# A half-sample Fourier basis with folded mirror tiles, and mask tables built two slots earlier, in a fused attention and long-convolution kernel

## The chip, the cores and the metric

The kernel runs on one core of one Trainium2 chip. The metric is the device time of one execution in microseconds (us). The granted clock is the share of PE's full clock that the profile shows as allowed. Engines are PE (TensorE), PEld (its weight loads), DVE (VectorE), ACT (ScalarE), POOL (GpSimd) and SP (SyncE).

A ratio below is the mean time of one kernel's fast runs over that of the other kernel's fast runs of the same rounds, so it is not quite the ratio of the medians quoted beside it. Brackets hold its 95% interval. An execution counts as slow when it is over 1.5% above the fastest of the same kernel.

## The reference

```python
# q, k, v: (4, 8, 768, 64); heads are "retrieval" (causal) or "stream" (4 sinks + window of 64)
scores = np.where(mask, scale * q @ k.T, -1e9);  a = softmax(scores)
x = (a @ v).transpose(0, 2, 1, 3).reshape(4, 768, 512)
proj = x @ w_proj;  x1, x2, x3 = split(proj, 3)              # 512 columns each
X2 = rfft(x2, axis=1);  H = rfft(filter_fft, axis=0)         # length 768
y = x1 * irfft(X2 * H) * x3
out = y @ w_out
```

## The kernel before

Sixteen pairs of heads (four batches of four) go through slots `n` = 0 to 15. In each slot the attention of one pair runs beside steps of the convolution of the batch before. Up to `n == 4` the engines' queues keep the order of the code. From slot 5 on a scheduler places what is emitted for PE, DVE and ACT, and it may put an instruction ahead of older ones when its operands allow. GpSimd and SyncE keep the order of the code throughout.

The Fourier transform is a matrix product. Tokens t and t+384 are added and subtracted, which leaves 3 tiles of 128 rows for each spectrum tile. So there are 6 output tiles x 3 matmuls = 18 forward matmuls a batch. The filter's spectrum tables HA and HB come from the same transform, straight from PSUM with a scale.

```python
psum = ctx.enter_context(tc.tile_pool(name="psum", bufs=4, space=bass.MemoryType.PSUM))   # 4 bank pairs
# ...
def emit_kinds():                        # which of three mask kinds, 128x3x256
    nc.vector.tensor_copy(out=kinds[:, 0:2], in_=code)
    nc.vector.tensor_copy(out=kinds[:, 2, 0:128], in_=code[:, 1, 0:128])
    nc.vector.memset(kinds[:, 2, 128:256], 2.0)
def emit_mask(h):                        # one table for each head
    nc.vector.tensor_scalar(out=mask[:, h], in0=kinds, scalar1=least[:, h:h + 1], scalar2=None, op0=ALU.is_ge)
# ...
def setup_steps():                       # filter tables, cut into steps by yield
    # fold = sum and difference of the filter's halves (DVE) ... yield
    ps = emit_forward(fold, ((0, 0), (1, 0)))
    for out_, in_, w in (...):           # four ACT copies with a scale: HA[:, 0], HB[:, 0]
        nc.scalar.activation(out=out_, in_=in_, func=AF.Copy, scale=scales[:, w:w + 1])
    put(nc.scalar, HA[0:1, 0, 1, :], ps[0:1, 1], 1.0)
    yield
    # tile 1: three DVE scales; yield; tile 2: one DVE and one ACT scale
# ...
for m in range(NM):                      # moe: x2 = projection, then sums and differences of the halves
    # 8 matmuls, x2s = ACT copy of the bank
    nc.vector.tensor_add(x2[:, 0, m, :], x2s[:, 0], x2s[:, 1])
    nc.vector.tensor_sub(x2[:, 1, m, :], x2s[:, 0], x2s[:, 1])
# ...
if n == BIASED:                          # BIASED = 4: the fifth pair's slot
    emit_turn(state[n - 2]); emit_values(last); emit_norm(last)
    emit_kinds(); emit_mask(0); emit_mask(1)
    next(setup); emit_turn(last); next(setup)
    emit_masking(st, 0); emit_chunks(st, 1); gates.append(moe(b - 1, last["xT"]))
    # ...
if n < 2 * BIASED:                       # slots 5 to 7
    emit_mask(2 * hp); emit_mask(2 * hp + 1)
```

The softmax here doesn't subtract the row's maximum and nothing guards it: scores larger than these inputs give would overflow.

Of the kernel before, what the change touches and what calls it, by code (L numbers as in the profile page):

```python
# [44 lines left out]
def kernel(  # L45
# [81 lines left out]
    def emit_prep(st):  # L127
        st["qkT"] = qkT = asb.tile([128, 2, S], BF16, name="qkT", bufs=3)
        if st["n"] < BY_PE:
            ps = bank_pair("qkT_ps", BF16)  # L130
            for a in range(2):
                for t in range(NT):
                    nc.tensor.transpose(ps[:, a, t * 128:(t + 1) * 128],
                                        st["bf"][:, a, t].rearrange("p hh d -> p (hh d)"), identity)
                if st["n"] == 0:
                    emit_blank(6 if a else 3)
            dst = qkT.rearrange("d a (p t) -> d a p t", t=NT)
            src = ps[:, :, 0:S].rearrange("d a (t p) -> d a p t", t=NT)
            if st["n"] == 0:
                for a in range(2):  # L140
                    nc.vector.tensor_copy(out=dst[:, a], in_=src[:, a])
            elif st["n"] <= BIASED:
                nc.vector.tensor_copy(out=dst, in_=src)
            else:
                nc.scalar.copy(out=dst, in_=src)
            return
        st["turn"] = nc.sync.dma_start_transpose(
            out=qkT.rearrange("p a (t s) -> p (a t) s", t=NT),
            in_=st["bf"].rearrange("p a t hh d -> p (a t hh d)"))
# [6 lines left out]
    def emit_blank(count):  # L156

        for i in range(count):
# [12 lines left out]
    tcol = const.tile([128, NM], FP32, name="tcol")  # L171
    nc.gpsimd.iota(tcol, pattern=[[128, NM]], base=0, channel_multiplier=1,
                   allow_small_or_imprecise_dtypes=True)
# [6 lines left out]
    nc.gpsimd.iota(par, pattern=[[0, 1]], base=0, channel_multiplier=1)  # L180
    nc.vector.tensor_scalar(out=par, in0=par, scalar1=1, scalar2=None, op0=ALU.bitwise_and)

    scales = const.tile([128, 4], FP32, name="scales")
    nc.gpsimd.memset(scales[:, 0:2], 2.0 / S)
    nc.gpsimd.memset(scales[:, 2:3], -2.0 / S)
    nc.gpsimd.memset(scales[0:1, :], 0.0)
    nc.gpsimd.memset(scales[0:1, 1:2], 1.0 / S)
    nc.gpsimd.memset(scales[0:64, 3:4], -2.0 / S)
    nc.gpsimd.memset(scales[64:128, 3:4], 2.0 / S)
    tfrac = const.tile([128, NM], FP32, name="tfrac")  # L190
    nc.vector.tensor_scalar(out=tfrac, in0=tcol, scalar1=1.0 / S, scalar2=None, op0=ALU.mult)
    quarter = const.tile([128, 1], FP32, name="quarter")
    nc.vector.memset(quarter, ETA * (S // 4))


# [14 lines left out]
    if n_sink:  # L210
# [3 lines left out]
        pattern=[[0, 2], [1, 128]], channel_multiplier=-1,  # L214
    )

    turns = msb.tile([128, NM, HS], I32, name="turns", tag="P")
# [8 lines left out]
    for m in range(NM):  # L226
        nc.vector.scalar_tensor_tensor(out=angle[:, m], in0=turns[:, m], scalar=-float(S),
                                       in1=angle[:, m], op0=ALU.mult, op1=ALU.add)
    nc.vector.tensor_scalar(out=size.bitcast(I32), in0=angle.bitcast(I32), scalar1=0x7fffffff,
                            scalar2=None, op0=ALU.bitwise_and)  # L230
    for out_, in_ in ((G[:, 1:4:2], angle[:, :, 0:256]), (G2[:, :, :, 64:128], angle[:, :, 256:384])):
        nc.scalar.activation(out=out_.rearrange("p r m f -> p m r f"), in_=in_.rearrange("p m (r f) -> p m r f", r=2), func=AF.Sin,
                             scale=-ETA)
    for out_, in_ in ((G[:, 0:4:2], size[:, :, 0:256]), (G2[:, :, :, 0:64], size[:, :, 256:384])):
        nc.scalar.activation(out=out_.rearrange("p r m f -> p m r f"), in_=in_.rearrange("p m (r f) -> p m r f", r=2), func=AF.Sin,
                             scale=-ETA, bias=quarter)
    emit_prep(state[0])
# [71 lines left out]
    def setup_steps():  # L309
        filt = state["filt"]  # L310
        fold = msb.tile([128, 2, NM, DM], BF16, name="fold", tag="y", bufs=2)
        nc.vector.tensor_add(fold[:, 0], filt[:, 0:NM, :], filt[:, NM:NT, :])
        nc.vector.tensor_sub(fold[:, 1], filt[:, 0:NM, :], filt[:, NM:NT, :])
        yield

        def put(engine, out, in_, w):
            if engine is nc.scalar:
                engine.activation(out=out, in_=in_, func=AF.Copy, scale=w / S)  # L318
            else:
                engine.tensor_scalar(out=out, in0=in_, scalar1=w / S, scalar2=None, op0=ALU.mult)  # L320


        ps = emit_forward(fold, ((0, 0), (1, 0)))
        for out_, in_, w in ((HA[:, 0, 0, :], ps[:, 0], 1), (HA[:, 0, 1, :], ps[:, 0], 0),
                             (HB[:, 0, 0, :], ps[:, 1], 2), (HB[:, 0, 1, :], ps[:, 1], 0)):
            nc.scalar.activation(out=out_, in_=in_, func=AF.Copy, scale=scales[:, w:w + 1])
        put(nc.scalar, HA[0:1, 0, 1, :], ps[0:1, 1], 1.0)
        yield
        ps = emit_forward(fold, ((2, 1), (3, 1)))
        put(nc.vector, HA[:, 1], ps[:, 0, None, :].to_broadcast([128, 2, DM]), 2.0)  # L330
        put(nc.vector, HB[:, 1, 0, :], ps[:, 1], -2.0)
        put(nc.vector, HB[:, 1, 1, :], ps[:, 1], 2.0)
        yield
        put(nc.vector, HA[:, 2], emit_forward(fold, ((4, 0), (5, 1))), 2.0)
        yield
        nc.scalar.activation(out=HB[:, 2], in_=emit_forward(fold, ((6, 0), (7, 1))), func=AF.Copy, scale=scales[:, 3:4])
        yield
# [71 lines left out]
    def emit_turn(st):  # L409
        if st["n"] < BY_PE or st["pair"][1] == HP - 1:  # L410
            ps = bank_pair("xt_ps", BF16)[:, 0, 0:S]
            for i in range(NT):
                nc.tensor.transpose(ps[:, i * 128:(i + 1) * 128],
                                    st["attn"][:, i].rearrange("p hh d -> p (hh d)"), identity)
            nc.vector.tensor_copy(out=st["xT"][:, st["pair"][1], :], in_=ps)  # L415
        else:
            nc.sync.dma_start_transpose(
                out=st["xT"][:, st["pair"][1], :].rearrange("p (t s) -> p t s", t=NT),
                in_=st["attn"].rearrange("p t hh d -> p (t hh d)"))


    def moe(b, xT):
        x2 = msb.tile([128, 2, NM, DM], BF16, name="x2")
        for m in range(NM):
            ps = bank_pair("x2_ps")
            for half in range(2):
                for cc in range(NC):
                    nc.tensor.matmul(ps[:, half, :], lhsT=xT[:, cc, half * HS + m * 128:half * HS + (m + 1) * 128],  # L428
                                     rhs=wproj[:, cc, DM:2 * DM],
                                     start=(cc == 0), stop=(cc == NC - 1))  # L430
            x2s = msb2.tile([128, 2, DM], BF16, name="x2s")
            nc.scalar.copy(out=x2s, in_=ps)  # L432
            nc.vector.tensor_add(x2[:, 0, m, :], x2s[:, 0], x2s[:, 1])
            nc.vector.tensor_sub(x2[:, 1, m, :], x2s[:, 0], x2s[:, 1])
            yield
        P = msb.tile([128, 3, 2, DM], BF16, name="P")
# [38 lines left out]
        def multiply(t, X):  # L475
            if t == 2:
                swapped = msb.tile([128, 2, DM], BF16, name="swapped")
                nc.sync.dma_start(out=swapped[0:64], in_=X[64:128])
# [10 lines left out]
        for t in range(3):  # L489
            X = msb2.tile([128, 2, DM], BF16, name="X", bufs=3)  # L490
            ps = emit_forward(x2, ((0, 0), (1, 1)), G2) if t == 2 else emit_forward(x2, ((2 * t, t), (2 * t + 1, t)))
            nc.scalar.copy(out=X, in_=ps)
# [113 lines left out]
    for n, (b, hp) in enumerate(pairs):  # L606
        if hp == 0:
            xT = msb.tile([128, NC, S], BF16, name="xT", bufs=2)
        st, last, nxt = state[n], state.get(n - 1), state.get(n + 1)
        st["xT"] = xT  # L610
        if n == MANUAL:
# [10 lines left out]
        if n < BIASED:  # L622
# [5 lines left out]
            else:  # L628
                setup = setup_steps()
                next(setup)  # L630
            emit_chunks(st, 1)
            if last:
# [6 lines left out]
            if n == 1:  # L639
                emit_doubles()  # L640
            continue
        if n == BIASED:
            emit_turn(state[n - 2])
            emit_values(last)
            emit_norm(last)
            emit_kinds()
            emit_mask(0)
            emit_mask(1)
            next(setup)
# [3 lines left out]
            emit_chunks(st, 1)  # L653
            gates.append(moe(b - 1, last["xT"]))
            gate_step()
# [27 lines left out]
        if hp == 0:  # L683
            gates.append(moe(b - 1, last["xT"]))
        if n != 2 * BIASED - 1:
# [14 lines left out]
    emit_turn(last)  # L700
    gates.append(moe(B - 1, xT))
    while gates:
# [38 lines left out]
```

## Time and profile before

| | before |
|---|---|
| median, range (the three runs before the prediction) | 214.45 us, 212.71 to 214.8 |
| profiled run | span 210.5 us, clock 0.992 of full speed |
| busy PE / DVE / ACT / POOL | 192.6 / 158.6 / 147.7 / 71.1 us |
| first x2 projection / first x1 projection on PE | 40.03 / 50.41 us |

In the lines of single instructions the columns are start, us, engine, line, operation, output and inputs, shapes, count, and in brackets the idle time before and what ended it.

### The profile page before, as it was taken

How to read it: one execution, taken by the hardware profiler on the slowest of the kernel's cores; microseconds unless marked ns; L12 is line 12 of the kernel's file. 1: busy time of each engine (PE TensorE's matmuls, PEld its weight loads, DVE VectorE, ACT ScalarE, POOL GpSimd, SP SyncE). 2: the span in 40 equal slices, each digit the busy share in tenths (PEclk: the TensorE clock that was granted, in tenths of full speed). 3: DMA queues.
4: the chain of work that ended last, by engine and by line, in shares of the span. 5: the costliest groups of instructions: out<-in, count | busy, mean ns of one | idle time of the engine just before them, and what ended most of it. 6: DMA issues, size and time to landing. Idle time of an engine off the chain costs nothing.

```text
span 210.5 us, 4337 instructions
## 1 busy us (share of the span) xinstructions
PE 192.6 (91%) x1763; PEld 106.2 (50%) x1763; DVE 158.6 (75%) x254; ACT 147.7 (70%) x183; POOL 71.1 (34%) x110
## 2 busy tenths in 40 slices
PE   7889998898969989999979999999899999999991
PEld 2346766444536546454536455545464654555540
DVE  6647877996899598996997777868975854686370
ACT  7798886896783777598857888789668246634621
POOL 6689365902482077255261520830000000000000
PEclk9999999999978999999999999999999999999999
DMA  5999998998999999997979799961403330022426
GB/s 154 251 311 234 292 271 202 184 199 158 216 196 180 222 206 180 229 241 133 219 137 205 162 213 242 246 114 23 90 0 111 118 112 0 3 50 91 186 73 250
DMA packets 89940, 35.29 MB, mean 168 GB/s; under 512 B 80320, under 2 KB 86464, under 8 KB 89920
## 3 DMA queue, kind: packets, MB, share of 16 engines
q1 hardware_dynamic: 87024, 32.13, 70.8%
q0 software_dynamic: 2896, 2.88, 8.6%
q8 instruction: 14, 0.23, 0.5%
q14 instruction: 6, 0.05, 0.1%
HBM read 24.65 MB, written 6.29 MB: 147 GB/s over the span
## 4 chain that ended last, share of the span: by engine, by line
PE 53%; DVE 24%; DMA 7%; ACT 6%; SPq 3%; POOL 3%; issue 2%; ACTq 0%; DVEq 0%; POOLq 0%
PE x_ps L444 17%; PE out_ps L533 9%; PE x_ps L428 8%; DMA qk_f<-in_k_dram 7%; PE c_ps L460 6%; PE att L395 5%; PE sc L362 4%; PE X_ps L301 3%; DVE pT L384 3%; DVE P L483 3%; SPq L95 3%; DVE attn L406 3%; ACT pT L377 3%; DVE mask L272 2%; DVE m L484 2%
## 5 line engine op out<-in xcount | busy, mean ns | idle before, releaser
L377 ACT ACTIVATE pT<-sc 128x1024 bf16<-128x1024 f32 x96 | 82.8, 922 | 16.3 <-PE sc L362 12.9
L444 PE MATMUL x_ps<-xT,wproj 128*128 128x384 bf16 x256 | 47.2, 334 | 3.6 <-DVE y L498 2.1
L115 POOL CAST qk_bf<-qk_f 128x768 bf16<-128x768 f32 x31 | 28.9, 939 | 63.1 <-DMA qk_f<-in_q_dram 55.8
L384 DVE TENSOR_TENSOR pT<-pT,mask 128x1024 bf16<-128x1024 bf16 x36 | 28.7, 797 | 12.0 <-ACT pT L377 12.0
L444 PEld LDWEIGHTS <-wproj 128*128 128x128 bf16 x256 | 24.8, 100 | 23.4 <-issue 7.7
L362 PE MATMUL sc<-qkT 64*128 64x512 bf16 (+3 forms) x256 | 28.0, 307 | 5.4 <-DVE xT L415 2.3
L395 PEld LDWEIGHTS <-pT 128*128 128x128 bf16 x672 | 23.1, 97 | 2.5 <-DVE pT L384 0.3
L395 PE MATMUL att<-v_aug,pT 128*128 128x65 bf16 x352 | 23.7, 193 | 0.0
L428 PE MATMUL x_ps<-wproj,xT 128*128 128x512 bf16 x96 | 22.1, 379 | 0.4 <-ACT HAB L318 0.2
L533 PE MATMUL out_ps<-wout,y 128*128 128x512 bf16 x92 | 21.8, 379 | 0.3 <-ACT pT L377 0.2
L452 ACT CAST x1s<-x_ps 128x768 bf16<-128x768 f32 x16 | 12.8, 801 | 11.7 <-PE x_ps L444 10.4
L395 PE MATMUL att<-v_far,pT 128*128 128x65 bf16 x320 | 20.7, 193 | 0.0
L362 PEld LDWEIGHTS <-qkT 64*128 64x128 bf16 x256 | 9.7, 94 | 19.5 <-issue 13.9
L347 POOL TENSOR_TENSOR v_far<-v_aug,vmask 128x520 bf16<-128x520 bf16 x16 | 18.6, 1163 | 1.3
L460 PE MATMUL c_ps<-Gi,P 128*128 128x384 bf16 x96 | 18.3, 326 | 0.2
L301 PE MATMUL X_ps<-x,G 128*128 128x512 bf16 x72 | 16.9, 380 | 0.1
L432 ACT CAST x2s<-x_ps 128x1024 bf16<-128x1024 f32 x12 | 12.2, 1015 | 6.6 <-PE x_ps L428 6.1
L115 POOL CAST v_aug<-v_f 128x768 bf16<-128x768 f32 x16 | 15.1, 942 | 3.2 <-DMA v_f<-in_v_dram 3.2
L465 DVE TENSOR_TENSOR conv<-evs,c_ps 128x384 bf16<-128x384 f32 x16 | 8.8, 550 | 9.1 <-ACT evs L463 9.1
L406 DVE TENSOR_TENSOR attn<-att,rec 128x768 bf16<-128x768 f32 x16 | 15.3, 956 | 0.5
L543 ACT COPY o_sb<-out_ps 128x1024 f32<-128x1024 f32 x9 | 9.1, 1012 | 9.0 <-PE out_ps L533 8.9
L428 PEld LDWEIGHTS <-xT 128*128 128x128 bf16 x96 | 9.0, 98 | 11.1 <-issue 1.2
(94 smaller groups left out, 235.7 us busy)
## 6 DMA issues: line engine op xcount, KB each, us to landing
qk_f<-in_q_dram SPq DMA_DIRECT2D x16, 384.0 KB, 6.5
qk_f<-in_k_dram SPq DMA_DIRECT2D x16, 384.0 KB, 6.5
v_f<-in_v_dram SPq DMA_DIRECT2D x16, 384.0 KB, 5.5
out_dram<-o_sb SPq DMA_DIRECT2D x9, 512.0 KB, 2.9
wproj<-in_moe_w_proj_dram POOLq DMA_DIRECT2D x3, 512.0 KB, 9.9
out_dram<-o_last SPq DMA_DIRECT2D x5, 256.0 KB, 2.5
swapped<-X SPq DMA_DIRECT2D x8, 128.0 KB, 2.8
filt<-in_moe_filter_fft_dram POOLq DMA_DIRECT2D x1, 768.0 KB, 10.7
```

The source lines that it names most:

```text
L115: nc.gpsimd.tensor_copy(out=out, in_=in_)
L301: nc.tensor.matmul(ps[:, u, :], lhsT=matrix[:, t, m, :], rhs=src[:, r, m, :], start=(m == 0), stop=(m == NM - 1))
L347: nc.gpsimd.tensor_mul(v_far, v_aug[:, 0:4], vmask[:, hp, :, :, None].to_broadcast([128, 4, 2, 65]))
L362: nc.tensor.matmul(sc[:, hh, n * 128:(n + cnt) * 128], lhsT=qkT[rows, 1, j * 128:(j + 1) * 128], rhs=qkT[rows, 0, i * 128:(i + cnt) * 128] ...
L377: nc.scalar.activation(out=pT[:, :, c, 0:w], in_=sc[:, :, 0:w], func=AF.Exp, scale=SCALE)
L384: nc.vector.tensor_mul(near, near, which)
L395: nc.tensor.matmul(att[:, hh, 65 * i:65 * i + 65], lhsT=st["pT"][:, hh, c, 128 * n:128 * n + 128], rhs=st["v_far" if i >= j + 2 else "v_au ...
L406: nc.vector.tensor_mul(st["attn"].rearrange("p i hh d -> p hh i d"), rows[:, :, :, 0:64], rec[:, :, :, None].to_broadcast([128, 2, NT, 64]))
L428: nc.tensor.matmul(ps[:, half, :], lhsT=xT[:, cc, half * HS + m * 128:half * HS + (m + 1) * 128], rhs=wproj[:, cc, DM:2 * DM], start=(cc = ...
L444: nc.tensor.matmul(ps[:, s, 0:HS], lhsT=wproj[:, cc, part * DM + cb * 128:part * DM + (cb + 1) * 128], rhs=xT[:, cc, s * HS:s * HS + HS], ...
L460: nc.tensor.matmul(ps[:, r, 0:HS], lhsT=P[:, t, u, ch], rhs=Gi[:, tile_no], start=(n == 0), stop=(n == 2))
L533: nc.tensor.matmul(ps[:, n, :], lhsT=y[:, cb, (i + n) * 128:(i + n + 1) * 128], rhs=wout[:, cb, :], start=(cb == 0), stop=(cb == NC - 1))
```

## The change

There are three intents. (1) With angles taken at half samples, rows that mirror each other have equal cosines and opposite sines. The first and the reversed third tile of x2 can then be added and subtracted once, and 18 forward matmuls become 12 slots of the array. The price is one sum and one difference on DVE a batch, one reversed copy a pair on POOL, and filter tables that need a rotation (ACT multiplies one part out of PSUM, DVE multiplies and adds the other). (2) `kinds` and the first two masks move from the fifth pair's slot to the end of the third pair's slot. (3) The start is adapted: a few constants and one warming matmul less. The new `sums` and the old `swapped` also share buffers with `x2s`.

```diff
         for t in range(2):
+            ps = emit_forward(fold, ((2 * t, t), (2 * t + 1, t)))
+            halves(0, t, ps[:, 0])                    # ACT: real_parts = ps * factor
+            halves(1, t, ps[:, 0])
+            whole(HA[:, t, 0, :], 0, t, ps[:, 1])     # DVE: ps * factor + real_parts
+            whole(HB[:, t, 1, :], 1, t, ps[:, 1])
+            nc.vector.tensor_copy(out=HA[:, t, 1, :], in_=HA[:, t, 0, :])
+            nc.vector.tensor_scalar(out=HB[:, t, 0, :], in0=HB[:, t, 1, :], scalar1=-1.0, ...)
+            if t == 0:
+                nc.scalar.activation(out=HA[0:1, 0, 1, :], in_=ps[0:1, 1], func=AF.Copy, scale=1.0 / S)
+            yield
# ... tile 2: four halves; yield; four wholes
             nc.sync.dma_start_transpose(out=st["xT"]..., in_=st["attn"]...)
+            emit_back(st)                             # the same behind the turn by PE
+    def emit_back(st):
+        nc.gpsimd.tensor_copy(out=st["back"][:, st["pair"][1], :, ::-1], in_=halves[:, :, 256:HS])
# ... in moe, after the third tile:
+                nc.vector.tensor_add(sums, x2[:, :, 0, :], x2[:, :, 2, :])
+                nc.vector.tensor_sub(x2[:, :, 0, :], x2[:, :, 0, :], x2[:, :, 2, :])
# ... forward: per output tile one matmul on x2's middle tile, one (or two of 64 columns) on the folded tile
             if n == 1:
                 emit_doubles()
+            elif n == 2:
+                emit_kinds()
+                emit_mask(0)
+                emit_mask(1)
             continue
         if n == BIASED:
             emit_norm(last)
-            emit_kinds()
-            emit_mask(0)
-            emit_mask(1)
             next(setup)
```

## The prediction

> **What bounds the kernel now.** I read the engine shares and slices of the page first, then the chain that ended last, then busy times by stretch, then PE's own waits, then single instructions in order of time. The page:
>
> ```profile
> PE 192.6 (91%) x1763; PEld 106.2 (50%) x1763; DVE 158.6 (75%) x254; ACT 147.7 (70%) x183; POOL 71.1 (34%) x110
> ...
> PE   7889998898969989999979999999899999999991
> ...
> DVE  6647877996899598996997777868975854686370
> ```
>
> PE is the fullest engine, but not everywhere: its dips (slices 8, 10, 20) fall where DVE shows 9. So I cut the span where the limit changes (stretch; then busy us with instruction counts for PE, weight loads, DVE, ACT, POOL; clock; DMA share; GB/s):
>
> ```profile
> 0.00:28.70 28.70, 24.41 (x261) 14.34 (x261) 19.86 (x38) 24.23 (x31) 19.75 (x48) 1.00 1.03 245
> 28.70:50.40 21.70, 19.73 (x202) 10.92 (x203) 19.73 (x34) 17.39 (x23) 10.28 (x15) 1.00 1.01 203
> 50.40:80.00 29.60, 26.00 (x267) 14.87 (x267) 24.14 (x34) 21.70 (x27) 13.94 (x16) 0.94 1.10 204
> ...
> 95.00:108.00 13.00, 11.45 (x104) 5.80 (x100) 10.95 (x17) 10.35 (x13) 4.89 (x7) 1.00 0.99 177
> 108.00:138.00 30.00, 29.79 (x290) 16.18 (x291) 24.36 (x38) 23.72 (x30) 11.95 (x15) 1.00 1.02 198
> 138.00:151.00 13.00, 12.13 (x111) 6.42 (x109) 10.87 (x18) 11.23 (x14) 2.04 (x2) 1.00 0.37 75
> 151.00:178.20 27.20, 26.91 (x227) 14.91 (x226) 17.08 (x31) 15.18 (x20) 0.00 (x0) 1.00 0.22 70
> 178.20:182.30 4.10, 4.10 (x21) 1.87 (x20) 2.24 (x5) 2.82 (x3) 0.00 (x0) 1.00 0.01 4
> ```
>
> What is to be seen: up to 28.7 us the chain is loads of q and k (two links of 7.07 and 7.64 us of DMA). From 28.7 to 50.4 the chain is almost wholly DVE, which is busy 19.73 of 21.70 us. From 50 to 108 PE and DVE take turns. From 108 to the end PE is full (29.79 of 30.00, 26.91 of 27.20), but for 138 to 151. The forward transforms of the four batches lie at 51.7 to 57.6, 96.6 to 101.9, 140.3 to 145 and 178.2 to 182.3: one in a DVE-limited place, one mixed, one nearly PE-bound, one purely PE-bound.
>
> [...]six forward matmuls take 1.31 us on the chain, 218 ns each, though the group's mean of 380 ns contains the pipeline. [...]four 64-row score matmuls of 512 columns span 0.55 us, as two full ones would[...]. [...]694 ns for 1024 bf16 elements from SBUF, 550 ns for 384 with one operand in PSUM. [...]one mask multiply takes 1.54 us at 92.39 beside 0.69 us elsewhere, and a 406 ns table build took 2086 ns.
>
> **The change, part by part.** The groups that it touches:
>
> ```profile
> L301 PE MATMUL X_ps<-x,G 128*128 128x512 bf16 x72 | 16.9, 380 | 0.1
> ...
> L485 DVE TENSOR_TENSOR P<-P,m 128x1024 bf16<-128x1024 bf16 x12 | 8.3, 694 | 0.2
> ...
> L320 DVE TENSOR_SCALAR HAB<-X_ps 128x1024 bf16<-128x1024 f32 (+1 forms) x4 | 3.6, 942 | 0.0
> ...
> L326 ACT ACTIVATE HAB<-X_ps,scales 128x512 bf16<-128x512 f32 x4 | 2.4, 687 | 1.8 <-PE X_ps L301 1.8
> ```
>
> A. PE. The 72 forward matmuls become, for each batch, 4 + 4 full ones (tiles 0 and 1) and 2 full plus 4 of 64 columns (tile 2). If the two 64-column halves run together these fill 12 slots in place of 18: 6 x 0.218 = 1.3 us a batch, 5.2 us in all. If they run one after the other, 14 slots: 0.87 us a batch, 3.5 us in all. I take 1.2 us[...].
>
> B. DVE, each batch: one sum and one difference over 128x1024 bf16. They have the shape of the 694 ns row, and start 0.60 us apart in a row of such work: 1.2 us a batch, 4.8 us in all.
>
> C. POOL: 16 reversed copies of 256 elements. A 768-element cast takes 0.82 us, 1.07 ns an element, so about 0.27 + 0.1 = 0.37 us each, 6 us in all. POOL is busy 34% and idles for 55.8 us on q loads, so its own time is free; where such a copy lies beside DVE work it may lengthen it, at most some 0.3 us each time.
>
> D. The filter tables, once, in the DVE stretch. DVE goes from 3.6 us to eight multiply-adds with PSUM ([...]0.68 us for 512 elements, 0.62 in a row), four short bf16 operations (0.2) and four tiny ones (0.12): 5.0 + 0.8 + 0.5 = 6.3, so 2.7 us more. ACT goes from 4 x 0.6 + 0.57 + 1.11 = 4.1 to 8 x 0.6 + 0.57 = 5.4, so 1.3 more, in the place (47 to 50 us) where it idles for 1.58.
>
> E. The mask tables. In the middle of the DVE stretch stand
>
> ```profile
> 36.90 0.55 DVE L267 COPY kinds<-code 128x512 bf16<-128x512 bf16 x1
> 37.37 0.18 DVE L268 COPY kinds<-code 128x128 bf16<-128x128 bf16 x1
> 37.53 0.17 DVE L269 MEMSET kinds<- 128x128 bf16 x1
> 37.73 1.23 DVE L272 TENSOR_SCALAR mask<-kinds,least 128x768 bf16<-128x768 bf16 x2
> ```
>
> 38.88 - 36.90 = 2.0 us on the path. They go to about 27.6 us, where DVE idles for 0.63 and then 0.50 us: 1.1 us vanish, 0.9 us push the 29.25 copy of qkT. Here I choose 1.1 us gained.
>
> F. Start: four constants and three small iotas on POOL before its 1.23 us idle, two tiny sines on ACT before its 1.00 us idle, one warming matmul less. All lies under the loads: 0.
>
> **The sum by place.** 0 to 28.7: 0. 28.7 to 57: E gives -1.1; D's DVE part and B's 1.2 add 3.9, of which the last multiply-adds and the sums meet DVE's 1.89 us idle at 50.4 and its 0.94 at 53.3 (2.8 us); A gives -1.2 on PE, of which I count half, as DVE leads there: -1.1 + 1.1 - 0.6, about -0.6. Batch 1 (95 to 108): A's 1.2 against B's 1.2, with DVE idle 0.38 + 1.53 us just before its products: -0.5. Batch 2: PE is full before and after, DVE has 2.1 us free in 13: -1.0. Batch 3: at the tail PE is bound, but the new sums make x2's last tile usable about 1.2 us later while the first x1 projection lasts 1.3; the middle-tile matmuls can go first, and some wait stays: -0.7. Contention from C: +0.4. Together -2.4 us: 214.45 - 2.4 = **212.0 us**, a ratio of 0.989.
>
> **Rivals.** (i) DVE takes over. Its total rises by 4.8 + 2.7 = 7.5 us to 166 of 210 us, and it is already full from 28.7 to 50.4 and from 100 to 109. For it speaks PE's longest wait after 80 us:
>
> ```profile
> PE x_ps L444 <- DVE y L498: 2.1, 2, 1.3
> ```
>
> a wait for DVE products, which B pushes back. Against it: DVE has 10 us free in 151 to 178 and 2 in most forward stages. If it won, the 5.2 us of PE would only become idle time and the kernel would take 214 to 216. (ii) Everything PE saves is collected: -5 us, 209 to 210, faster by over 2%. For it: PE is at 99% over 57 of the last 100 us. Against it: two of four forwards lie where PE is not the limit. (iii) POOL becomes a wait: it is strictly in order, the reversed copy waits for the turned attention, the casts of the next pair come behind it, and the single `back` buffer must be given up by the batch before. At batch 0 the copy of pair 3 comes at about 43.1 us (after the 41.30 product of 1.05) and is needed at 44.68, a margin of 1.6 us. A miss would cost 1 to 2 us there, giving 213 to 214. (iv) Column halves serialise: 1.7 us less gain, 213.
>
> **Range and chances.** From the sum, each of A, B, D and E is uncertain by about 1 us; instructions after the first five pairs are also placed by a scheduler, which may move any of them, 1 to 1.5 us either way; and the three runs before spread over 2.1 us. Added as squares, that is about 2.3 us: 209.2 to 215.0 should hold it 8 times in 10. Faster by over 2% needs under 210.2, that is rival (ii): 0.16. Slower by over 2% needs over 218.7, that is (i) with (iii): 0.05. Within 2%: 0.79.
>
> **What would show it.** A: PE's busy time falls by 3.5 to 5.2 us, and the two halves of a pair start within a few tens of ns. B: eight new DVE instructions of about 0.6 to 0.7 us, DVE busy near 166. C: POOL about 6 us busier, and no PE wait on `back`. D and E: no mask work between 36 and 39 us, and the last table multiply-add ending near 52 us; the stretch from 28.7 us to the first x1 projection (50.41 now) no longer than 1.5 us more. Tail: the last forward shorter than 4.1 us with a PE wait under 0.6 us. The prediction is wrong if DVE waits replace PE time at the second and third forward, if POOL holds back the third x2 tile, or if the scheduler reorders the tail.

## More of the kernel before

The before kernel was timed again on the chip of each batch of experiments. Its median there was 213.6 to 214.7 us. The batches ran on different chips, so kernels of different batches are compared only by their ratios.

The fence is from the before kernel, in order of time:

```profile
28.20 0.56 DVE L415 COPY xT<-xt_ps 128x768 bf16<-128x768 bf16 x1 [0.63 <-PE xt_ps L413]
29.25 1.76 DVE L143 COPY qkT<-qkT_ps 128x1536 bf16<-128x1536 bf16 x1 [0.50 <-PE qkT_ps L133]
...
32.66 0.22 DVE L405 RECIPROCAL rec<-att 128x12 f32<-128x12 f32 x1
...
35.76 0.23 DVE L405 RECIPROCAL rec<-att 128x12 f32<-128x12 f32 x1 [0.72 <-PE att L395]
...
39.34 2.09 DVE L272 TENSOR_SCALAR mask<-kinds,least 128x768 bf16<-128x768 bf16 x1
...
44.28 1.07 DVE L272 TENSOR_SCALAR mask<-kinds,least 128x768 bf16<-128x768 bf16 x3
...
46.54 0.74 DVE L272 TENSOR_SCALAR mask<-kinds,least 128x768 bf16<-128x768 bf16 x2
```

A `RECIPROCAL` opens the normalisation of a pair. The third pair's is at 32.66 and the fourth's at 35.76. The six later masks come after both, in three groups.

## The result, and the profile after

The changed kernel took 220.15 us (219.34 to 222.18, 4 runs) against 213.58 (212.0 to 214.8). The ratio is 1.0326 [1.022, 1.0433]: slower, where 212.0 was predicted. The page of the profiled run (span 218.3 us), in shares and slices:

```profile
PE 191.0 (87%) x1733; PEld 104.9 (48%) x1746; DVE 172.2 (79%) x274; ACT 148.4 (68%) x188; POOL 80.8 (37%) x127
...
PE   7599965779897877979869999999999999999992
...
DVE  8647899979999979789899866887997655596461
...
PEclk9969999699999999999999999999999999999999
```

PE fell by only 1.6 us and DVE rose by 13.6 us. PE has a new hole in slices 6 to 9 (27 to 49 us), and in slice 8 the granted clock falls with it (0.50 from 38.5 to 41.5 us). To see where the time went I cut both spans at the first x2 projection of each batch on PE (us, profiled runs):

| stretch | before | after | difference |
|---|---|---|---|
| start to batch 0 | 40.03 | 47.32 | +7.29 |
| batch 0 to 1 | 47.49 | 47.81 | +0.32 |
| batch 1 to 2 | 43.91 | 45.13 | +1.22 |
| batch 2 to 3 | 40.28 | 39.39 | -0.89 |
| batch 3 to end | 38.79 | 38.65 | -0.14 |
| span | 210.5 | 218.3 | +7.8 |

Nearly all of the loss is in the set-up. VectorE's queue there, in the changed kernel, in order of time:

```profile
28.22 0.81 DVE L277 COPY kinds<-code 128x512 bf16<-128x512 bf16 x1
...
29.92 1.60 DVE L282 TENSOR_SCALAR mask<-kinds,least 128x768 bf16<-128x768 bf16 x2
...
35.93 0.78 DVE L328 TENSOR_TENSOR turned<-trig,weight 128x4 f32<-128x4 f32 x1
36.63 0.15 DVE L329 SCALAR_TENSOR_TENSOR turned<-trig,weight 128x4 f32<-128x4 f32 x1
...
37.48 0.22 DVE L431 RECIPROCAL rec<-att 128x12 f32<-128x12 f32 x1
37.62 0.34 DVE L282 TENSOR_SCALAR mask<-kinds,least 128x768 bf16<-128x768 bf16 x1
...
38.76 0.87 DVE L282 TENSOR_SCALAR mask<-kinds,least 128x768 bf16<-128x768 bf16 x2
...
40.23 3.51 DVE L282 TENSOR_SCALAR mask<-kinds,least 128x768 bf16<-128x768 bf16 x3
43.66 0.22 DVE L431 RECIPROCAL rec<-att 128x12 f32<-128x12 f32 x1
```

All six later masks now stand ahead of the fourth pair's normalisation, which slips from 35.76 to 43.66. They are among the instructions that the scheduler may place, and with `kinds` ready from 29.9 us it pulled them forward. Not all of the delay is their doing. The third pair's normalisation has none of them ahead of it and is already 4.8 us late (37.48 for 32.66): `kinds` and the first two masks take 3.2 us at their new place (28.22 to 31.44), and behind them one sum of the filter's halves is stretched (1.57 us for 0.95) and the four `turned` products are new. From there to the fourth pair's normalisation it is 6.2 us in place of 3.1, so the six masks add some 3.1 us.

The first `turned` product needs 0.15 us by itself and took 0.78. What POOL did in those moments:

```profile
35.43 1.26 POOL L115 CAST qk_bf<-qk_f 128x768 bf16<-128x768 f32 x1 [0.23 <-DMA qk_f<-in_k_dram]
36.64 0.15 POOL L369 MEMSET v_aug<- 128x12 bf16 x1
36.69 0.86 POOL L115 CAST v_aug<-v_f 128x768 bf16<-128x768 f32 x1
```

The product ends at 35.93 + 0.78 = 36.71, the cast beside it at 35.43 + 1.26 = 36.69: VectorE's instruction ends when the cast does, within 0.02 us. PE in the same time:

```profile
38.89 0.82 PE L439 MATMUL xt_ps<-identity,attn 128*128 128x128 bf16 x6 [2.85 <-DVE attn L432]
...
41.83 1.48 PE L311 MATMUL X_ps<-fold,G 128*128 128x512 bf16 x5
44.92 0.51 PE L439 MATMUL xt_ps<-identity,attn 128*128 128x128 bf16 x6 [1.61 <-DVE attn L432]
...
47.32 1.90 PE L463 MATMUL x_ps<-wproj,xT 128*128 128x512 bf16 x8
...
57.72 0.49 PE L484 MATMUL x_ps<-xT,wproj 128*128 128x384 bf16 x2 [0.67 <-ACT real_parts L336]
```

PE waits twice for a normalisation, and the first x1 projection starts at 57.72 instead of 50.41.

The fold itself does on PE what it was meant to do, at a price. The two 64-column halves of a pair start together:

```profile
62.76 0.38 PE L535 MATMUL X_ps<-x,G 128*128 128x512 bf16 x1
63.07 0.40 PE L541 MATMUL X_ps<-sums,G 128*64 128x512 bf16 x1
63.07 0.40 PE L541 MATMUL X_ps<-x,G 128*64 128x512 bf16 x1
63.41 0.39 PE L535 MATMUL X_ps<-x,G 128*128 128x512 bf16 x1
63.73 0.40 PE L541 MATMUL X_ps<-x,G 128*64 128x512 bf16 x1
```

But each change between whole and half width costs about 0.1 us here: these starts are 0.31 to 0.34 us apart, where whole matmuls in a row (59.02, 59.23, 59.45) start 0.22 apart. With four changes a batch, six slots less are worth some 1.31 - 0.45 = 0.9 us, an estimate from these starts. Batch 2 gains 0.89 us (table above).

### The profile page after: what moved, and what is told of

Same layout as the page of the kernel before.

```text
span 218.3 us, 4333 instructions
## 1 busy us (share of the span) xinstructions
PE 191.0 (87%) x1733; PEld 104.9 (48%) x1746; DVE 172.2 (79%) x274; ACT 148.4 (68%) x188; POOL 80.8 (37%) x127
## 4 chain that ended last, share of the span: by engine, by line
PE 50%; DVE 29%; ACT 7%; DMA 5%; issue 3%; POOL 3%; SPq 1%; ACTq 0%; DVEq 0%; POOLq 0%
PE x_ps L484 12%; PE x_ps L463 10%; PE out_ps L587 8%; PE c_ps L500 6%; DVE pT L410 5%; PE sc L388 4%; PE att L421 4%; DVE attn L432 4%; DMA qk_f<-in_k_dram 4%; DVE mask L282 2%; DVE P L523 2%; ACT pT L403 2%; DVE P L525 2%; DMA out_dram<-o_sb 2%; DVE m L524 2%
## 5 line engine op out<-in xcount | busy, mean ns | idle before, releaser
L484 PE MATMUL x_ps<-xT,wproj 128*128 128x384 bf16 x256 | 45.8, 327 | 4.5 <-DVE y L552 2.2
L410 DVE TENSOR_TENSOR pT<-pT,mask 128x1024 bf16<-128x1024 bf16 x36 | 31.7, 881 | 8.2 <-ACT pT L403 8.1
L452 POOL COPY back<-xT 128x256 bf16<-128x256 bf16 x16 | 8.3, 519 | 75.7 <-DMA xT<-attn 50.3
L388 PE MATMUL sc<-qkT 64*128 64x512 bf16 (+3 forms) x256 | 29.5, 311 | 5.8 <-DVE xT L441 2.5
L115 POOL CAST qk_bf<-qk_f 128x768 bf16<-128x768 f32 x31 | 29.2, 958 | 13.6 <-DMA qk_f<-in_q_dram 8.2
L421 PE MATMUL att<-v_aug,pT 128*128 128x65 bf16 x352 | 25.1, 197 | 1.9 <-DVE pT L410 1.9
L421 PEld LDWEIGHTS <-pT 128*128 128x128 bf16 x672 | 24.2, 100 | 4.8 <-DVE pT L410 2.4
L421 PE MATMUL att<-v_far,pT 128*128 128x65 bf16 x320 | 21.8, 197 | 0.0
L115 POOL CAST v_aug<-v_f 128x768 bf16<-128x768 f32 x16 | 16.3, 1020 | 0.7 <-DMA v_f<-in_v_dram 0.7
L463 PE MATMUL x_ps<-wproj,xT 128*128 128x512 bf16 x61 | 14.7, 380 | 0.3 <-DVE xT L441 0.2
L587 PEld LDWEIGHTS <-y 128*128 128x128 bf16 x92 | 8.6, 97 | 10.7 <-DVE conv L506 0.9
```

The lines of the kernel that those rows point to most:

```text
L115: nc.gpsimd.tensor_copy(out=out, in_=in_)
L388: nc.tensor.matmul(sc[:, hh, n * 128:(n + cnt) * 128], lhsT=qkT[rows, 1, j * 128:(j + 1) * 128], rhs=qkT[rows, 0, i * 128:(i + cnt) * 128] ...
L410: nc.vector.tensor_mul(near, near, which)
L421: nc.tensor.matmul(att[:, hh, 65 * i:65 * i + 65], lhsT=st["pT"][:, hh, c, 128 * n:128 * n + 128], rhs=st["v_far" if i >= j + 2 else "v_au ...
L463: nc.tensor.matmul(ps[:, half, :], lhsT=back[:, cc, half, :] if m == 2 else rows, rhs=wproj[:, cc, DM:2 * DM], start=(cc == 0), stop=(cc = ...
L484: nc.tensor.matmul(ps[:, s, 0:HS], lhsT=wproj[:, cc, part * DM + cb * 128:part * DM + (cb + 1) * 128], rhs=xT[:, cc, s * HS:s * HS + HS], ...
```

## The experiments

My first theory was that the move of the masks and the longer table chain each delay the set-up. The rivals were that the folded transform itself is the cost (DVE's added work), or GpSimd's copies. Later the question became what the rest of the loss is made of. All kernels give right results except the two marked.

| run | what it is | median us | ratio |
|---|---|---|---|
| e1 | fold only, masks in the old place | 219.87 | 1.0293 [1.021, 1.0375] |
| e2 | before + masks moved only | 217.98 | 1.0201 [1.0123, 1.0279] |
| e3 | after + six later masks pinned to the end of slot 4 | 219.04 | 1.0279 [1.0218, 1.0341] |
| e5 | e1 + that pin | 219.46 | 1.0303 [1.0231, 1.0374] |
| e6 | e3 + last turn before the first table step | 219.98 | 1.0368 [1.0205, 1.0532] |
| e8 | e6, one-row fix on DVE | 221.70 | 1.0435 [1.032, 1.055] |
| e9 | e8 with both table steps ahead of the masks | 218.22 | 1.0174 [0.9916, 1.0432] |
| e10 | e3 without the fold | 218.72 | 1.0296 [0.9881, 1.0712] |
| e11 | e5 with the tables ahead of the masks | 216.99 | 1.0136 [1.0078, 1.0193] |
| e12 | e11 without the fold | 217.27 | 1.0168 [1.0095, 1.0241] |
| e13 | e11, reversed copies on ACT | 219.92 | 1.0278 [1.0229, 1.0327] |
| e14 | e11, rotation factors at the start | 217.12 | 1.0133 [1.0063, 1.0203] |
| e16 | e14 without the fold | 215.79 | 1.0133 [1.0037, 1.0229] |
| e17 | e14, last table on ACT (wrong result) | 215.06 | 1.0056 [0.9974, 1.0138] |
| e18 | e17 without the fold (wrong result) | 215.03 | 1.0061 [0.9983, 1.0138] |
| e19 | e14, masks in DVE's idle gaps | 217.32 | 1.0179 [1.0115, 1.0244] |
| e20 | e14, reversed copies behind the casts | 215.92 | 1.0039 [0.9947, 1.0132] |
| e21 | after, reversed copies behind the casts | 217.04 | 1.0157 [1.0077, 1.0236] |

### One part alone: e1 and e2

e1 is the changed kernel with the three mask lines back in slot 4. e2 is the kernel before with only this:

```diff
             if n == 1:
                 emit_doubles()
+            elif n == 2:
+                emit_kinds(); emit_mask(0); emit_mask(1)
# slot 4:
-            emit_kinds(); emit_mask(0); emit_mask(1)
```

> The folded basis alone: the first two mask tables stay where the kernel before has them. Theory M (the loss comes from the mask tables: once the shared pattern is built in the third pair's slot, the six later tables, which are placed by the scheduler, are pulled ahead of the fourth pair's normalisation on VectorE, 4.65 us of them between 37.6 and 43.7 us): 213 to 215 us, at most 1% above before, normalisation of the fourth pair within 2 us of where it was (36.0). Theory F (the loss comes from the fold: filter tables, turned factors, sums, reversed copies on GpSimd): 218 to 220 us.

> The kernel before with nothing changed but the place of the first two mask tables (end of the third pair's slot). Theory M: 216.5 to 219.5 us, with the six later tables again ahead of the fourth pair's normalisation, which starts at 40 us or later. Theory F: 212.5 to 214 us, as before.

Both are slower, by 2.9% and 2.0%. They do not add up to the change's 3.3%, because both spend in the same stretch. VectorE in e2, where nothing of the fold exists:

```profile
34.85 0.97 DVE L272 TENSOR_SCALAR mask<-kinds,least 128x768 bf16<-128x768 bf16 x1
35.75 0.22 DVE L405 RECIPROCAL rec<-att 128x12 f32<-128x12 f32 x1
35.89 1.07 DVE L272 TENSOR_SCALAR mask<-kinds,least 128x768 bf16<-128x768 bf16 x1
...
39.69 1.49 DVE L272 TENSOR_SCALAR mask<-kinds,least 128x768 bf16<-128x768 bf16 x2
41.10 0.22 DVE L405 RECIPROCAL rec<-att 128x12 f32<-128x12 f32 x1
```

So moving three lines of mask work costs 2.0% without any fold, and the six other masks go ahead of the fourth pair's normalisation (41.10 in place of 35.76). How much of the cost is theirs is not separated. When the first of them starts, at 34.85, VectorE is already 2.2 us later than at the third pair's normalisation before (32.66); the other 3.1 us come after it. No run pins these masks without the fold. In e1 the normalisations are on time (36.22), and still the first x2 projection comes at 45.02. ScalarE, PE and VectorE of e1, one line or two of each engine:

```profile
43.95 0.59 ACT L352 ACTIVATE HAB<-X_ps 1x512 bf16<-1x512 f32 x1 [5.16 <-DVE HAB L348]
...
44.59 0.50 PE L388 MATMUL sc<-qkT 64*128 64x384 bf16 x2 [4.95 <-ACT HAB L352]
...
37.89 2.42 DVE L278 COPY kinds<-code 128x128 bf16<-128x128 bf16 x1
...
42.31 1.40 DVE L339 SCALAR_TENSOR_TENSOR HAB<-X_ps,turned,real_parts 128x512 bf16<-128x512 f32 x2
```

Before, ScalarE alone released the first table's bank. Now the release goes through VectorE, whose queue holds `kinds` and the masks ahead of the multiply-adds: ScalarE's halves were ready at 38.78, the multiply-adds start at 42.31. PE waits 4.95 us for the bank. Some 2.2 us of this are bad timing, the one copy of `kinds` that took 2.42 us beside casts (0.18 before). In e5 the same copy takes 1.26 and PE still waits 3.90 us. Busy times in 40 to 45 us (stretch, then PE, PEld, DVE, ACT, POOL, clock, DMA share, GB/s), from e1:

```profile
40.00:45.00 5.00, 0.41 (x2) 0.10 (x1) 4.96 (x12) 1.05 (x2) 2.12 (x4) 0.74 1.21 199
45.00:50.00 5.00, 5.00 (x25) 2.51 (x24) 4.22 (x9) 3.60 (x6) 2.26 (x5) 0.58 1.26 217
```

PE stands still, its clock falls to 0.58 of full speed in the next 5 us, and eight x2 matmuls then take 3.59 us instead of 1.89. The clock was at 0.50 from 43 to 49 us. It fell near 42.4 us, 2.8 us into the wait, and in the changed kernel it fell near 38.5 us, within the wait of 2.85 us.

### Pinning, and the order of the turn: e3, e5, e6, e8

The pin takes the six masks out of the scheduler's hands:

```diff
-        if n < 2 * BIASED:
-            emit_mask(2 * hp); emit_mask(2 * hp + 1)
# end of slot 4:
+            for h in range(2, H):
+                emit_mask(h)
```

> The changed kernel whole, but the six later mask tables are emitted in the fixed order at the end of the fifth pair's slot, so that they can't be pulled forward. Theory M: 212 to 215 us, the fourth pair's normalisation before 39.5 us. Theory F: 218 us or more, since the fold is all still there.

> Folded basis, first two mask tables at the old place, six later ones fixed at the end of the fifth pair's slot. Theory M: 211.5 to 214.5 us, close to the previous run or a little below. Theory F: 218 us or more.

e3 brings the fourth normalisation from 43.7 back to 38.4 us, and the first x2 projection to 44.54. The time hardly moves (1.0279 against 1.0326, with intervals that overlap). e5 leaves e1 where it was. So with the fold in place the overtaking masks cost nothing that can be told apart; PE waits for the tables' bank in both (1.67 us in e3, 3.90 in e5). I then tried the last turn before the first table step (e6), and in e8 also the one-row fix on DVE instead of ACT:

```diff
             emit_norm(last)
-            next(setup)
             emit_turn(last)
+            next(setup)
```

```diff
-                nc.scalar.activation(out=HA[0:1, 0, 1, :], in_=ps[0:1, 1], func=AF.Copy, scale=1.0 / S)
+                nc.vector.tensor_scalar(out=HA[0:1, 0, 1, :], in0=ps[0:1, 1], scalar1=1.0 / S, scalar2=None, op0=ALU.mult)
```

> The pinned version of the changed kernel (219.0 us), with one more edit: in the fifth pair's slot the fourth pair's turned attention is copied before the filter tables are begun, not after their first step. Theory S (the filter tables' new chain PE, ScalarE, VectorE stands in fixed-order queues between the fourth pair's normalisation and its x2 projection): the copy of xT moves from 43.7 to about 39.8 us and the first x2 projection from 44.5 to 41 to 43 us; time 216 to 218 us. Theory P (the loss comes from the sums and the reversed copies of every batch): no change, 218 to 220 us.

> As the previous run, and the one-row correction of the first table goes from ScalarE, where it waits for VectorE's copy (1.68 us in the pinned version, 5.16 us in the fold-only one), to VectorE behind that copy. Theory S: ScalarE never waits for the tables, PE's wait for the score bank shrinks below 1 us, 215 to 217.5 us. Theory P: 218 to 220 us.

Both ideas failed. In e6 the turned pair is copied at 39.36 in place of 43.72 (e3), as expected, but x2 comes at 44.24 (44.54 in e3). The filter's transform on PE moves back to 39.15 us (38.22 in e3), because the turn in front of it waits for the normalisation, and x2 waits for the tables' bank as before. The one-row fix is where the wait was recorded, but e8 is no faster. Its profile is already 2.55 us late at the fourth pair's normalisation (40.08, against 37.53 in e6), ahead of the fix, so it says little about the fix itself.

### Tables ahead of the masks: e9, e11, e12, e13, and e10

```diff
             emit_norm(last)
-            emit_kinds(); emit_mask(0); emit_mask(1)
             next(setup); emit_turn(last); next(setup)
+            emit_kinds(); emit_mask(0); emit_mask(1)
```

e9 does this to e8 (where the turn stands first), e11 does it to e5. e12 and e10 take the fold out of e11 and e3 (18 matmuls, no sums, no copies; basis and tables kept). e13 has the copies on ScalarE.

> As the previous run, but the first two mask tables are back in the fifth pair's slot, behind the filter tables and ahead of the first masking, so that nothing is added to VectorE before 36 us. Theory S: the normalisation of the fourth pair at 35.5 to 36.5 us, 213.5 to 216.5 us, the fastest of these. Theory P: 218 to 220 us.

> The pinned version with the half-sample basis and its filter tables, but without the fold of the batches: 18 full forward matmuls a batch again, no sums, no reversed copies. Theory S: the set-up alone costs what is lost, 217 to 219.5 us. Theory P: 213 to 215 us, as before.

> Changed kernel with one order in the fifth pair's slot: normalisation, first filter tables, turn of the fourth pair, second filter tables, and only then the mask tables (the six later ones fixed at the end of the slot); the forward transform of the filter is not put behind the normalisation as in the two turn-first runs. Theory S (x2 starts late because the banks of the filter's forward transform come free only when VectorE, which has mask work ahead of it, has read them): the first x2 projection at 40 to 42 us (40.03 before, 43.1 to 47.4 in the versions so far), time 214 to 217 us. If x2 starts there and the time stays at 218 or more, the loss lies after 57 us and S is only half of it.

> The previous run without the fold of the batches (18 forward matmuls, no sums, no reversed copies). Its difference from the previous run is the worth of the fold once the set-up is out of the way. Theory S with a fold that pays: 215 to 217 us, slower than the previous run by 1 to 3 us. Theory D (after 57 us the fold's sums on VectorE cost more than its matmuls save): 212.5 to 215 us, faster than the previous run by 1 to 3 us.

> The tables-ahead version with the 16 reversed copies on ScalarE in place of GpSimd. If GpSimd's waits for the turned attention (75.7 us in the changed kernel) hold back its casts, or the copies slow VectorE: faster by 1 us or more. If not: within 1 us, or slower, since ScalarE gets about 6 us more work and waits in order.

e9's interval is too wide to say anything. e11 against e5 is the same work in another order, 1.0136 against 1.0303, and their intervals do not touch: about half of the loss was the order in the set-up. e12 shows no loss or gain by the fold that could be told apart (1.0168 against 1.0136). e10's interval holds everything. e13 is worse as a whole, and I first read it as clearing GpSimd. That was too quick, as e20 shows below.

### Factors early, and what is left: e14, e16 to e19

In e11 the copy behind the first multiply-adds took 1.73 us beside casts (0.28 by itself), and PE waited for the bank. e14 computes the four tiny `turned` factors at the start of the kernel instead of ahead of the third pair's normalisation. The first line is PE in e11, the second is PE in e14:

```profile
42.57 0.34 PE L388 MATMUL sc<-qkT 64*128 64x384 bf16 x2 [2.91 <-ACT HAB L352]
```

```profile
39.94 0.34 PE L388 MATMUL sc<-qkT 64*128 64x384 bf16 x2 [1.46 <-ACT HAB L352]
```

> The tables-ahead version with the four tiny products of the turned factors moved from the fourth pair's slot (where they took 0.6 to 1.9 us of VectorE beside GpSimd's casts) to the start, where VectorE waits for loads. Theory S: 0.5 to 1.5 us faster than the tables-ahead version; the third pair's normalisation at 32.7 us as before the change.

The set-up is now on time in the profile (x2 at 40.21, x1 at 50.61 us, against 40.03 and 50.41 before), and yet the ratio is 1.0133: the 0.5 to 1.5 us expected over e11 (1.0136) did not come. The shorter wait is also in part luck. The copy took 0.28 us in this profile; in e20, whose set-up is the same code, it took 1.64 us beside casts again, and x2 came at 42.38. The rest was looked for by taking work away. e16 is e14 without the fold; e17 writes the last table by ScalarE; e18 does both; e19 spreads the masks over VectorE's idle gaps.

```diff
# e17
-            whole(HA[:, 2, u, :], 0, 2 + u, ps[:, u])
-            whole(HB[:, 2, u, :], 1, 2 + u, ps[:, u])
+            nc.scalar.activation(out=HA[:, 2, u, :], in_=ps[:, u], func=AF.Copy, scale=turned[:, 0, 1, 2 + u:3 + u])
+            nc.scalar.activation(out=HB[:, 2, u, :], in_=ps[:, u], func=AF.Copy, scale=turned[:, 1, 0, 2 + u:3 + u])
```

```diff
# e19: kinds, masks 0 and 1 ahead of the first table step again,
#      masks 2 and 3 ahead of the second, 4 to 7 after the second x2 step
```

> e14 (tables ahead of the masks, rotation factors early) without the fold: 18 forward matmuls, no sums, differences and reversed copies. If VectorE's added time in the stretch from 50 to 111 us is what the remaining 1.3% is made of, taking 1.4 us of sums and differences per batch out moves it: first normalisation of the fifth pair near 56 us, the one of the tenth (110.9 in e14) near 109.5, the ratio near 1.007. If the fold pays for itself on TensorE (the prediction's step A), this run is slower than e14, near 1.02. If both balance, 1.013 again.

> Wrong result on purpose: e14, with the last table tile written by ScalarE straight from the bank (four copies with a scale) in place of the four VectorE multiply-adds of 2.71 us. If the VectorE work queued at 50 to 57 us is the cause, the first product of the spectrum (58.66 us in e14, 54.24 before) comes 2 to 2.7 us earlier and the ratio goes to about 1.003. If it is not, ratio stays at 1.010 to 1.015.

> Wrong result on purpose: e17 without the fold, so that VectorE has about the work of the kernel before in every batch. If VectorE's work is the whole of the remainder, ratio 0.995 to 1.003. If the remainder comes from the basis itself (table chain, extra ScalarE halves of 4.9 us, banks held), ratio stays above 1.007.

> Right result, a try at a better version: e14 with the masks put where VectorE idled in e14: kinds and the first two before the first table step (gap of 1.37 us at 36.3), two before the second step (gap of 1.12 at 40), four before the third pair of x2 sums (gap of 0.94 at 47). If only the total VectorE work between 28 and 57 us counts, about 2 us are won: ratio near 1.004. If masks ahead of the table steps delay the tables' bank once more, the first x2 projection goes from 40.2 to 41.5 or later and the ratio stays at 1.013 or rises.

e16 equals e14: the fold is again worth nothing that can be told apart. e17 and e18 come to 1.006, so the last multiply-adds may be part of the rest, but the intervals overlap e14's. In e17's profile, a slow run, the first spectrum product comes at 58.30, not the expected 2 to 2.7 us ahead of e14's 58.66. e19 is a miss: with masks ahead of the table steps the x2 projection came at 41.48, as the second of its expectations had it. But the stretches between x2 projections, from the profiled runs, told more than the totals:

| kernel | start to batch 0 | 0 to 1 | 1 to 2 | 2 to 3 | to end |
|---|---|---|---|---|---|
| before | 40.03 | 47.49 | 43.91 | 40.28 | 38.79 |
| e2, no fold | 45.62 | 47.97 | 43.80 | 40.28 | 39.13 |
| e16, no fold | 40.21 | 49.45 | 43.40 | 40.28 | 38.46 |
| after | 47.32 | 47.81 | 45.13 | 39.39 | 38.65 |
| e11 | 42.84 | 48.73 | 45.14 | 39.39 | 38.70 |
| e14 | 40.21 | 50.49 | 47.16 | 39.39 | 38.65 |
| e13, copies on ACT | 41.63 | 51.29 | 44.17 | 42.12 | 38.69 |
| e20, copies late (slow run) | 42.38 | 50.84 | 43.62 | 39.51 | 38.65 |
| e21, copies late (slow run) | 48.80 | 47.18 | 43.86 | 39.74 | 38.62 |

From batch 2 to 3, where PE is the limit, the fold saves 0.89 us: 40.28 or 40.29 in all five fast profiles without it, 39.39 in all nine with it on GpSimd. From batch 1 to 2 it loses: 43.4 to 44.2 without it, 45.1 to 47.5 with it. (e18, in a slow run, breaks both: 47.15 and 40.42.) And e13, with GpSimd freed of the copies, has 44.17 there.

The nine with the fold fall into two groups: 45.1 to 45.2 (the changed kernel, e3, e6, e11) and 47.1 to 47.5 (e1, e5, e8, e14, e19). PE waits the same 2.2 us for the product `y` in all nine. In the second group alone the granted clock then falls to half (in e14 from 110.2 to 113.4 us), and that goes with the other 2 us: the 16 matmuls behind the wait take 4.04 to 4.44 us there and 2.76 us in the first group. So the fold loses 1 to 1.7 us here, and some 2 us more where the clock falls.

### GpSimd's order: e20 and e21

VectorE, GpSimd and PE of the changed kernel in the second forward:

```profile
109.94 1.30 DVE L523 TENSOR_TENSOR P<-X,HAB 128x1024 bf16<-128x1024 bf16 x1
111.17 1.31 DVE L524 TENSOR_TENSOR m<-X,HAB 128x1024 bf16<-128x1024 bf16 x1
112.51 1.42 DVE L525 TENSOR_TENSOR P<-P,m 128x1024 bf16<-128x1024 bf16 x1
113.86 0.94 DVE L552 TENSOR_TENSOR y<-x1s,x_ps 128x768 bf16<-128x768 bf16 x1
...
107.58 0.67 POOL L452 COPY back<-xT 128x256 bf16<-128x256 bf16 x1 [6.75 <-DMA xT<-attn]
108.20 2.51 POOL L115 CAST qk_bf<-qk_f 128x768 bf16<-128x768 f32 x2
...
114.86 2.76 PE L484 MATMUL x_ps<-xT,wproj 128*128 128x384 bf16 x16 [2.18 <-DVE y L552]
```

GpSimd's fixed order makes the casts of the next pair wait behind a reversed copy, which waits 6.75 us for a DMA. When they are let go, they lie one behind another on VectorE's spectrum products. These take 1.3 to 1.4 us in place of 0.68, and PE waits 2.18 us for the product after them. (The kernel before has stretched products here too, 1.54 us at 100.06 and 1.30 at 109.06, but not three in a row ahead of `y`; PE's wait there is 1.3 us.) The last two runs keep all work and put the copies of DMA-turned tiles behind the next slot's casts:

```diff
# emit_turn, the branch with the DMA
-            emit_back(st)
+            backs.append(st)
# each slot, after emit_cast(state[n + 2]) and emit_v(state[n + 1]); and once more after the loop
+        while backs:
+            emit_back(backs.pop(0))
```

> e14 with the reversed copies of the tiles that a DMA turns put behind the casts of the next pair in GpSimd's fixed order, so that no cast stands behind a copy that waits for a DMA. If GpSimd's order is what makes the second forward expensive (in the changed kernel the casts held up until 108.2 us lie on VectorE's products, 1.30 us each in place of 0.68, and TensorE waits 2.18 us for the product after them), the stretch from the first x2 projection of batch 1 to that of batch 2 goes from 47.16 us to about 44, its wait for that product to 1.2 or less, and the ratio to 1.000 to 1.008. If only VectorE's amount of work counts, the stretch stays at 45 or more and the ratio at 1.013.

> The changed kernel with that one edit (its set-up untouched). GpSimd's order the cause: stretch of batch 1 from 45.13 us to about 44, ratio from 1.033 to about 1.027; the set-up still costs its 7 us (first x1 projection near 57 us). Not the cause: stretch 45 or more, ratio unchanged.

VectorE in e20, the same products, and then PE's waits for `y` between 90 and 138 us (in total, times, longest):

```profile
108.62 0.69 DVE L523 TENSOR_TENSOR P<-X,HAB 128x1024 bf16<-128x1024 bf16 x1
109.22 0.68 DVE L524 TENSOR_TENSOR m<-X,HAB 128x1024 bf16<-128x1024 bf16 x1
109.94 0.69 DVE L525 TENSOR_TENSOR P<-P,m 128x1024 bf16<-128x1024 bf16 x1
```

```profile
PE x_ps L484 <- DVE y L552: 0.2, 1, 0.2
```

The stretch fell to 43.62 us (e20, from 47.16 in e14) and 43.86 (e21, from 45.13 in the changed kernel), as the first expectation of each had it. About 2 us of e20's gain are the clock fall that e14 had and e11 (45.14) had not. Both profiles fell in slow runs, and no fast profile of either exists. A slow run is longer, so it is not likely to have made the stretch shorter, but no fast profile confirms it. The ratios are 1.0039 and 1.0157, about 0.9 and 1.7 points under the parents'. They rest on three and four fast runs, and their intervals still overlap the parents'; e20 can't be told from the kernel before any more. So GpSimd's order as the cause here is well supported, but not shown. That e21 won more than the 1.27 us of this stretch (its expected 1.027 was too high) isn't explained by its profile, whose set-up is still late; its fast runs have no profile.

No version beat the kernel before.

## Why the prediction was wrong

The predicted 212.0 us was 8 us too low. By its own steps:

**E, the masks, failed, and in its sign.** It said "1.1 us vanish, 0.9 us push the 29.25 copy of qkT". Alone, the move costs 2.0% (e2), some 4 us. The step looked at idle time at the new place and not at what becomes possible once `kinds` exists. Six more masks, which the before kernel had in three groups from 39.34 us on, went ahead of a normalisation on which PE waits: 0.34 + 0.87 + 3.51 = 4.7 us in the changed kernel. And the moved work itself took 3.2 us at its new place, where 0.9 was to remain. With the fold in place, though, neither taking the move back (e1, 1.0293) nor pinning the six masks (e3, 1.0279) wins anything that can be told from 1.0326: the next step alone is enough for the loss. The "no mask work between 36 and 39 us" that should have shown the step right was not met either.

**D, the tables, was sized nearly right and placed wrong. This is the step that failed most.** Eight multiply-adds of 743 ns on VectorE were predicted at 0.68. (The page of the kernel before gives that rate: with one operand in PSUM, 384 elements take 550 ns and 768 take 956, so 128 more than 384 add some 0.13 us, an estimate.) But the sum treated D as 2.7 us of work that meets idle time. It was a new link in the release of a PSUM bank, behind other work in a fixed queue: PE waits 4.95 us in e1 and 1.46 in e14. That a different order of the same work (e11 against e5) takes about half of the loss away shows it. e1, which keeps D and the fold and drops E, loses 2.9%, and e12 finds the fold itself worth nothing that can be told apart. The last multiply-adds, "ending near 52 us", ended at 60.6.

**C, "its own time is free", failed.** GpSimd's share of busy time was no measure. What counts is its order: copies wait for a DMA and the casts behind them come at a bad moment. The step allowed "at most some 0.3 us each time" for work beside a copy, and left out the casts held up behind it, beside which 0.68 us products took 1.3 to 1.4. The copies themselves took 8.3 us for the predicted 6. Rival (iii) named the fixed order, but looked for a wait on `back`. The cost came through VectorE, as far as e20 and e21 can say.

**B held in size.** Sums and differences take 685 and 708 ns. The DVE total of near 166 was met in e3 (166.1), e11 (165.0) and e14 (166.6). The changed kernel's 172.2 is the same work as e3's 166.1; the rest is stretching.

**A was right where PE is the limit and not elsewhere.** PE's busy time fell by 3.8 us in e11 and by 1.6 in the changed kernel (3.5 to 5.2 predicted). A slow clock stretches it at times in the changed kernel (0.50 from 38.5 to 41.5 us) and in the one before (0.80 from 62 to 68 us), so this total says little. Batch 2 gained 0.89 us for the predicted 1.0. That is near in part by luck: the step took 1.2 us of its 1.3, 0.1 less, and the changes of width take some 0.45. Batch 1 lost 1.22 where 0.5 was to be gained: this is rival (i), and the wait the prediction quoted for it, PE on the product `y`, is the very one that grew, from 1.3 to 2.18 us in one place. (PE also waits 0.5 us there on the new difference.) Batch 3's tail gained 0.14 for 0.7, and not by the fold: the same basis without it (e10, e12, e16) ends in 38.45 to 38.52 us, with it in 38.63 to 38.70. Why the tail collects nothing isn't known. So the fold nets to about nothing in the changed kernel, and e12 and e16 agree.

**The range was too narrow.** The scheduler was given 1 to 1.5 us "either way"; in e2 the masks that it moved add some 3.1 us to the delay of a normalisation, though what they alone cost in time was not measured. And a waiting PE could cost twice: the idle stretch, and the slow clock after it (0.58 in e1 from 45 to 50 us), which the prediction left out.

**What stays open.** The stretch from batch 0 to 1 takes 50.5 us in e14 and 50.8 in e20, for 47.5 before. In e14 VectorE is full there from 50.5 to 57 us (6.50 of 6.50; 3.82 before, 5.19 in e20). The clock does not explain it: e14 has 0.86 from 68 to 80 us, but the kernel before has 0.80 from 62 to 68, and e20 has full clock from 50.5 to 88. e17 points to the last four multiply-adds, but its interval does not settle it.

## What to carry to other kernels

Before moving an instruction into an idle gap, ask what it unlocks: a table that is ready earlier lets everything that depends on it overtake. In an engine that keeps its order, put an instruction that waits for a DMA behind those that do not, even if the engine is two thirds idle (supported here by e20, 47.16 to 43.62 us, and e21, 45.13 to 43.86 us, not shown). And when a step that one engine did alone becomes a chain of two, count what stands ahead of it in the second engine's queue, not the length of the step.

## What the traces show of the hardware

- VectorE beside GpSimd's casts and multiplies: in the changed kernel a 0.15 us product took 0.78 us, and products of 0.68 us took 1.30 to 1.42 us.
- The same over several instructions: in e1 a copy on VectorE that takes 0.18 us in the before kernel took 2.42 us, from 37.89 to 40.31, while GpSimd ran two casts, a memset and a third cast back to back until 40.25.
- Matmuls of 512 columns start 0.31 to 0.34 us apart at each change between whole and 64-column width in the changed kernel, and 0.22 us apart without one.
- The granted clock fell 2.8 us into a wait of PE (e1), 2.4 us (the changed kernel) and 1.9 us (e14, a wait of 2.2 us); the same wait of 2.2 us in e11 had no fall after it.
- A reversed copy of 256 bf16 elements on GpSimd took 0.39 to 0.40 us at the least, 0.52 us on average, in the changed kernel.
